# Banded attention and a split-precision feed-forward layer: the planner's port rule, four product parts and single sums

## The chip, the cores and the metric

The kernel runs on one core of one Trainium2 chip. The metric is the device time of one execution in microseconds. Three runs of the kernel before took 921.04, 918.73 and 920.68 us, median 920.68. The engines are TensorE (PE; its weight loads are PEld), VectorE (DVE), ScalarE (ACT), GpSimd (POOL) and SyncE (SP), which issues the DMAs.

## The reference

Attention over a band of 64 keys (8 batches, 8 heads, 576 positions, head size 64), then a feed-forward layer over the 4608 tokens:

```python
scores = scale * np.matmul(q, k.transpose(0, 1, 3, 2))
rel = pos[:, None] - pos[None, :]
scores = np.where((rel >= 0) & (rel < 64), scores, -1000000000.0)
scores = scores - np.max(scores, axis=-1, keepdims=True)
attn = np.exp(scores)
attn = attn / (np.sum(attn, axis=-1, keepdims=True) + 1e-09)
x = np.matmul(attn, v)              # -> (4608, 512)
...
h = x @ w_in                        # (512, 2048)
g = np.where(h >= 1, h, np.where(h <= -1, 0.0, (h + 1) ** 2 / 4))
return g @ w_out                    # (2048, 512)
```

## The kernel before

The tokens are cut into nine tiles of 512. Attention runs in steps of 128 tokens, four to a tile, some tiles ahead of the feed-forward layer. A step is: loads, scores on TensorE (L401), mask (L418) and maximum (L422) on VectorE, exponentials on ScalarE (L429), the inverse of the sum (`den`, L436 and L437) on VectorE, the normalization (`sm`, L441) on VectorE or GpSimd, twelve transposes of 32x32 blocks on VectorE (L447, two times six), and the value product on TensorE (L476).

Matrix operands of the feed-forward layer are split in two: a rounded high part and the low rest, so every product is three matmuls (high x high, high x low, low x high). Tiles 0 and 1 compute h = x w_in directly (L860, one block f of 128 columns of h at a time, 16 blocks to a tile). From tile 2 on (`PLAIN = 2`), two blocks f are computed together as one pair n by seven products of sums in place of eight (L812): sums of parts of x (L529), their high parts (`xs`, L259 casts) and low parts (`xs`, L541), and sums of parts of the weights. The weight sums (`add_sums`, eight of them in two halves c) are computed once, during tile 1: `sum_whole` (L724, two operations), `sum_sums` (L733, four), rounding on ScalarE, `sum_low` (L743). They are written to DRAM (`kept`) and come back for every tile as rings of weights (`wr`, L783).

A pair's products stand in two banks of PSUM, `ps_h`. They were issued in two pieces: 24 matmuls (products 0 to 3), then 18 (products 5, 6 and 4). From the banks, h is put together in SBUF: `h_copy` (L257 or L259) and five sums `h_add` (L828), three after the first piece and two after the second. The second piece waits for the copy and all of the first three sums. The last sum and the last copy free the banks for the next pair. Then, for each block: relu and square on ScalarE (L872, L877; the square on VectorE at times, L879), the gate on VectorE (L884), rounding on ScalarE (`gh`, L889), the low part on GpSimd (`gl`, L894), and twelve matmuls of the second layer (L911) into four `acc` banks.

No order is written out by hand. Every operation is handed to a planner (`Plan.add`) with a key, a cost in ns for each engine that may run it, what it follows, and which buffers it takes and gives back. `Plan.run` plays the kernel forward with these costs: of the operations that an engine could start soonest (within `PATIENCE` of it) it takes the one with the lowest key, and where two engines may run an operation, the one that could start it first gets it. What comes out is each engine's fixed instruction order. The costs are thus no times of the chip but decide the order; `tt(n)` gives those of sums, `hi(n)` those of rounding.

Of the kernel before, what the change touches and what calls it, by code (L numbers as in the profile page):

```python
# [10 lines left out]
F32 = mybir.dt.float32  # L11
# [29 lines left out]
W_LEAD = 0.57  # L41
W_FIRST = (20.54, -1.96, 1.46, 0.57, -0.16)
# [45 lines left out]
S_LATER = 2  # L88
B_KEY = 4 / 3
# [13 lines left out]
class Plan:  # L103
# [9 lines left out]
    def add(self, key, cost, do, after=(), takes=(), gives=(), lag=0):  # L113
        self.work.append((key, cost, do, set(after), takes, gives, lag))
        return len(self.work) - 1
# [16 lines left out]
    def run(self):  # L132
# [9 lines left out]
        turn = dict.fromkeys(self.pools, 0)  # L142

# [8 lines left out]
        for _ in self.work:  # L152
            best = None
            for e in engines:
                could = []
                for i, at in ready[e].items():
                    takes = self.work[i][4]
                    free = [self.pools[n][(turn[n] + takes[:j].count(n)) % len(self.pools[n])] for j, n in enumerate(takes)]
                    if None not in free:
                        could.append((max([at, idle[e]] + free), self.work[i][0], i, e))  # L160
# [5 lines left out]
            _, cost, do, _, takes, gives, lag = self.work[i]  # L166
            idle[e] = self.end(e, at, cost[e])
            ends[i] = idle[e] + lag, e
# [17 lines left out]
def banded_attention_then_ffn(ctx: ExitStack, tc: tile.TileContext, q, k, v, w, masks, out, dims):  # L186
# [142 lines left out]
    def add_weights(f, nf, unit):  # L329
# [3 lines left out]
        key = f * W_STEP - (W_FIRST[f] if f < len(W_FIRST) else W_LEAD) + .5 * nf * unit  # L333
# [217 lines left out]
    def tt(n, k=1):  # L551
        return dict(DVE=100 * k + 1.5 * n, Pool=200 * k + 2.3 * n)

    def hi(n):
        return dict(ACT=90 + .84 * n, DVE=65 + 1.05 * n)

    def add_build(t, r, due, x0, x1):
        i0 = add(due, tt(2 * SB), lambda e: x_sums(t, r, 0, e), [x0, x1], takes=["u"])
        xs = i0
        for j in range(1, 4):  # L560
            xs = add(due, tt(2 * SB), lambda e, j=j: x_sums(t, r, j, e), [xs])
        ends = []
        for k in range(5):
# [6 lines left out]
            x = add(due, hi(n), lambda e, k=k: x_high(t, r, k, e), after, takes=[] if t in x_first else ["x"])  # L570
            x_first.setdefault(t, x)
            gives = [("u", i0)] if k == 1 else [("u", x0)] if k == 4 else []
            x = add(due, tt(n), lambda e, k=k: x_low(t, r, k, e), [x] + ends[-1:], gives=gives)
# [3 lines left out]
    def add_step(t, i):  # L577
# [44 lines left out]
        if s < SOON:  # L622
            for h in range(2):
# [9 lines left out]
                x = add(due + D_LATE[4], NORM[1], lambda e, h=h: att_normalize(s, h, e), [x])  # L633
# [21 lines left out]
        else:  # L655
# [5 lines left out]
            x = [add(due[h], NORM[0], lambda e, h=h: att_normalize(s, h, e), [x]) for h in range(2)]  # L661
# [55 lines left out]
    def sum_whole(n, c, eng):  # L717
        if n < 2:
# [4 lines left out]
        for i, w_ in enumerate(by_chunk(n)):  # L723
            engine[eng].tensor_tensor(  # L724
                out=t[:, 2 * i:2 * i + 2], in0=w_[:, 0, c].bitcast(F32), in1=w_[:, 1, c].bitcast(F32), op=ALU.add
            )

    def sum_sums(n, c, eng):
# [218 lines left out]
    def step(t):  # L947
        return NF * starts[t] / 384
# [180 lines left out]
```

## Time and profile before

The profiled execution took 920.28 us, of which 918.5 are its span.

| what | number |
|---|---|
| median of 3 runs (lowest, highest) | 920.68 us (918.73, 921.04) |
| profiled execution, its span | 920.28 us, 918.5 us |
| granted TensorE clock, mean | 0.987 |
| the chain that ended last | PE 64%, DVE 21%, ACT 6%, DMA 4%, issue 3%, POOL 2% |
| moved by DMA | 187.60 MB, mean 204 GB/s |

How to read the rows: a group of instructions has its line, engine, operation, out<-in, shapes and count, then busy us and mean ns of one, then the idle time before it and what ended it. A row of the timeline has start and length in us, and in brackets the idle time of the engine before it with its releaser. A window has its bounds and length, the busy time of PE, PEld, DVE, ACT and POOL with instruction counts, then the granted clock of TensorE as a share of full speed, the DMA share and GB/s. Lines are those of the kernel before; in the changed kernel the same code stands 8 to 13 lines lower.

### The profile page before, as it was taken

Reading aid. Unit: us, or ns where it says so; the run is one execution under the profiler, and the core shown is the slowest. Engines: PE = TensorE matmul, PEld = TensorE weight load, DVE = VectorE, ACT = ScalarE, POOL = GpSimd, SP = SyncE. Lnnn points to the kernel's source line nnn. Section 1 sums busy time; section 2 is a strip of 40 time slices with the busy share of each in tenths; the row PEclk is TensorE's granted clock in tenths of the full one; section 3 lists DMA queues with packets and bytes.
Section 4 is the critical chain, followed back from the end, with each engine's and each line's share of the span. In section 5 each row is a group of like instructions: output and inputs, shape, how many; then the busy total and the mean of one; then the engine's idle time right before and its main releaser. Section 6 shows DMA issues by size and latency. Waiting matters only on the chain.

```text
span 918.5 us, 20359 instructions
## 1 busy us (share of the span) xinstructions
PE 879.8 (96%) x7839; PEld 762.4 (83%) x7839; DVE 667.5 (73%) x1348; ACT 503.5 (55%) x1297; POOL 317.7 (35%) x305
## 2 busy tenths in 40 slices
PE   7799998989989999999999999999999999999998
PEld 5678886867878888888888898888788878998997
DVE  6999997799787568866787668866895678533331
ACT  7899955455464444644564446435644555434343
POOL 1000035667442425432353235422533343422222
PEclk9999999989998999999999999999999999999999
DMA  9991169366475657655776568556865564556531
GB/s 327 414 364 53 36 203 296 129 208 234 163 240 201 202 189 240 231 183 172 246 230 203 190 208 292 189 174 218 278 197 194 178 229 162 161 164 226 184 116 46
DMA packets 108033, 187.60 MB, mean 204 GB/s; under 512 B 8480, under 2 KB 49696, under 8 KB 107936
## 3 DMA queue, kind: packets, MB, share of 16 engines
q1 hardware_dynamic: 107648, 185.38, 60.5%
q8 instruction: 62, 1.02, 0.5%
q10 hardware_dynamic: 288, 0.92, 0.3%
q14 instruction: 35, 0.29, 0.1%
HBM read 162.15 MB, written 24.12 MB: 203 GB/s over the span
## 4 chain that ended last, share of the span: by engine, by line
PE 64%; DVE 21%; ACT 6%; DMA 4%; issue 3%; POOL 2%; SPq 0%; ACTq 0%; DVEq 0%
PE acc L911 30%; PE ps_h L812 22%; DVE ptd L447 6%; PE ps_h L860 6%; DVE a L884 3%; PE ps_a L476 2%; PE ps_a L401 2%; DVE h L828 2%; ACT a L872 2%; ACT sm L429 2%; DVE xs L259 2%; DVE half L733 2%; DVE u L529 2%; DMA kt<-in_k 2%; DMA kept<-half 1%
## 5 line engine op out<-in xcount | busy, mean ns | idle before, releaser
L911 PE MATMUL acc<-wts,gh 128*128 128x512 f32 x1154 | 363.0, 396 | 0.2 <-ACT o L257 0.2
L812 PEld LDWEIGHTS ps_h<-xs,wr 128*128 128x128 f32 x2352 | 296.1, 191 | 26.4 <-DVE h L828 18.2
L812 PE MATMUL ps_h<-xs,wr 128*128 128x256 f32 x2352 | 304.3, 285 | 14.0 <-DVE h L828 14.0
L894 POOL TENSOR_TENSOR gl<-a,gh 128x512 fp32r<-128x512 f32 (+1 forms) x130 | 171.1, 1320 | 316.2 <-ACT gh L889 299.2
L911 PEld LDWEIGHTS acc<-wts,gh 128*128 128x128 f32 x1154 | 208.3, 189 | 41.2 <-ACT o L257 0.6
L911 PE MATMUL acc<-wts,gl 128*128 128x512 f32 x577 | 225.2, 390 | 0.3 <-POOL gl L894 0.3
L828 DVE TENSOR_TENSOR h<-h,ps_h 128x256 f32<-128x256 f32 x280 | 116.7, 417 | 109.7 <-PE ps_h L812 80.8
L889 ACT CAST gh<-a 128x512 fp32r<-128x512 f32 (+1 forms) x149 | 89.6, 602 | 122.9 <-PE acc L911 93.2
L447 DVE STREAM_TRANSPOSE ptd<-sm 32x256 f32<-32x256 f32 x336 | 146.3, 435 | 8.0 <-POOL sm L441 2.2
L911 PEld LDWEIGHTS acc<-wts,gl 128*128 128x128 f32 x577 | 108.9, 189 | 24.5 <-POOL gl L894 0.7
L884 DVE SCALAR_TENSOR_TENSOR a<-a,h 128x512 f32<-128x512 f32 x112 | 86.5, 772 | 57.9 <-ACT a L877 56.9
L429 ACT ACTIVATE sm<-sm,nm 128x96 f32<-128x96 f32 (+1 forms) x256 | 93.1, 365 | 49.0 <-DVE nm L422 49.0
L860 PE MATMUL ps_h<-xh,wts 128*128 128x512 f32 (+1 forms) x296 | 91.9, 379 | 10.1 <-DVE a L884 7.8
L257 ACT COPY h<-ps_h 128x256 f32<-128x256 f32 x95 | 35.3, 371 | 118.5 <-PE ps_h L812 118.2
L877 ACT ACTIVATE a<-a 128x512 f32<-128x512 f32 (+1 forms) x140 | 86.3, 617 | 4.4
L872 ACT ACTIVATE a<-h 128x512 f32<-128x512 f32 x112 | 70.0, 625 | 10.2 <-DVE h L828 10.2
L860 PEld LDWEIGHTS ps_h<-xh,wts 128*128 128x128 f32 x296 | 55.4, 195 | 22.3 <-DVE a L884 9.6
L541 POOL TENSOR_TENSOR xs<-u,xs 128x256 fp32r<-128x256 f32 (+1 forms) x57 | 60.0, 1075 | 23.7 <-DVE xs L259 22.0
L724 POOL TENSOR_TENSOR half<-wts 128x256 f32<-128x256 f32 x18 | 13.5, 769 | 132.7 <-PE ps_h L860 126.6
L860 PE MATMUL ps_h<-xl,wts 128*128 128x512 f32 (+1 forms) x148 | 55.5, 375 | 0.9 <-DVE xl L489 0.9
L441 POOL TENSOR_TENSOR sm<-sm,den 128x384 f32<-128x384 f32 x30 | 32.3, 1082 | 66.3 <-DVE den L437 62.2
L429 ACT ACTIVATION_READ_ACCUMULATOR sm<-sm,nm 128x1 f32 x256 | 48.0, 188 | 0.0
(89 smaller groups left out, 763.8 us busy)
## 6 DMA issues: line engine op xcount, KB each, us to landing
wr<-kept SPq DMA_DIRECT2D x112, 512.0 KB, 4.6
wr<-kept SPq DMA_DIRECT2D x112, 384.0 KB, 3.8
vt<-in_v SPq DMA_DIRECT2D x72, 256.0 KB, 4.0
kt<-in_k SPq DMA_DIRECT2D x35, 384.0 KB, 5.4
raw<-in_w SPq DMA_DIRECT2D x12, 1023.8 KB, 10.3
qt<-in_q SPq DMA_DIRECT2D x36, 256.0 KB, 4.9
out<-o SPq DMA_DIRECT2D x33, 256.0 KB, 4.7
kept<-wts SPq DMA_DIRECT2D x48, 128.0 KB, 2.5
```

The costliest lines, as they stand in the source:

```text
L429: nc.scalar.activation(sm[:, p, :], (ps if masked else sm)[:, p, :], AF.Exp, bias=nm[:, p:p + 1], scale=scale if masked else 1.0, accum_ou ...
L447: nc.vector.transpose(dst[:, :, r], src[:, :, c * SQ:(c + 1) * SQ])
L541: engine[eng].tensor_tensor(out=x_target(t, r, k, 1), in0=x_source(t, r, k), in1=x_target(t, r, k, 0).bitcast(F32), op=ALU.subtract)
L812: nc.tensor.matmul(ps[:, c * 2 * SB:(c + 1) * 2 * SB], lhsT=r[:, part, cp, o], rhs=xo[k][:, xp, cp], start=i == 0 and c == 0 and j == 0 an ...
L828: nc.vector.tensor_tensor(out=h[:, to:to + 256], in0=h[:, of:of + 256], in1=ps[:, at:at + 256], op=ALU.add)
L860: nc.tensor.matmul(ps, lhsT=wts[f, 0][:, part, c * P:(c + 1) * P], rhs=x[:, c, r], start=(c == 0 and j == 0), stop=(c == NP - 1 and j == 2),)
L872: nc.scalar.activation(gs[t, f, r.start][0], phs[t, f, r.start], AF.Relu, bias=0.5, scale=0.5)
L877: nc.scalar.activation(a, a, AF.Square)
L884: nc.vector.scalar_tensor_tensor(out=a, in0=a, scalar=1.0, in1=ps, op0=ALU.min, op1=ALU.max)
L889: nc.scalar.copy(g[1], g[0])
L894: engine[eng].tensor_tensor(out=g[2], in0=g[0], in1=g[1].bitcast(F32), op=ALU.subtract)
L911: nc.tensor.matmul(acc[t, i][:, n], lhsT=g[:, sub], rhs=wts[f, 1][:, part, n], start=(q == 0 and j == 0), stop=(q == NF - 1 and j == 2 and ...
```

## The change

1. The planner gets a resource that VectorE and GpSimd share. Every GpSimd operation holds it, and every VectorE operation that is added with `shared=True`: sums of x, their high and low parts, normalizations of attention, squares, gates of tiles from 2 on, and the weight sums. Two holders don't overlap in the plan. The costs change with it: VectorE's sums from 100 + 1.5 n to 65 + 1.04 n ns, its rounding from 65 + 1.05 n to 30 + 0.6 n, the gate from 100 + 1.3 n to 65 + 1.04 n, GpSimd's sums from 2.3 n to 2.15 n.
2. The products of a pair come in four parts of 12, 12, 6 and 12 matmuls. The third part needs the copy and the first sum of h, the fourth all three. The third part is now product 4 (bank 0) alone, so the last copy follows it and not the last part.
3. `sum_whole` and `sum_sums` become six operations for the planner in place of two; the instructions are the same.
4. Three keys change: the second-layer weights of joint loads (`W_PAIR`), the pace of the weight sums (`S_PACE`, 2 for a sum in place of 2.67), and that of the third part (`X_KEY`).

```diff
+W_PAIR = 0, 2.0
+S_PACE = 2
+X_KEY = 1.3
...
     def run(self):
...
+        held = 0.0
...
                     if None not in free:
+                        if e == "Pool" or e == "DVE" and self.work[i][7]:
+                            free.append(held)
                         could.append((max([at, idle[e]] + free), self.work[i][0], i, e))
...
             idle[e] = self.end(e, at, cost[e])
+            if e == "Pool" or e == "DVE" and shared:
+                held = idle[e]
...
-        key = f * W_STEP - (W_FIRST[f] if f < len(W_FIRST) else W_LEAD) + .5 * nf * unit
+        key = f * W_STEP - (W_FIRST[f] if f < len(W_FIRST) else W_LEAD) + (W_PAIR[unit] if nf == 2 else .5 * unit)
...
     def tt(n, k=1):
-        return dict(DVE=100 * k + 1.5 * n, Pool=200 * k + 2.3 * n)
+        return dict(DVE=65 * k + 1.04 * n, Pool=200 * k + 2.15 * n)
 
     def hi(n):
-        return dict(ACT=90 + .84 * n, DVE=65 + 1.05 * n)
+        return dict(ACT=90 + .84 * n, DVE=30 + .6 * n)
...
-            x = [add(due[h], NORM[0], lambda e, h=h: att_normalize(s, h, e), [x]) for h in range(2)]
+            x = [add(due[h], NORM[0], lambda e, h=h: att_normalize(s, h, e), [x], shared=True) for h in range(2)]
...
-        key = step(1) + 2 * n * TMAX / 384 + (S_LATE if n < 2 else S_LATER)
+        key = step(1) + S_PACE * n + (S_LATE if n < 2 else S_LATER)
...
-            k = key + c * TMAX / 384
-            x0 = add(k, tt(2 * TMAX // 2, 2), lambda e, c=c: sum_whole(n, c, e), after, takes=["tmp"])
+            k = key + c * S_PACE / 2
+            xs = add(k, tt(2 * P), lambda e, c=c: sum_whole(n, c, 0, e), after, takes=["tmp"], shared=True)
+            x0 = add(k, tt(2 * P), lambda e, c=c: sum_whole(n, c, 1, e), [xs], shared=True)
...
-            x = add(k, tt(4 * P, 4), lambda e, c=c: sum_sums(n, c, e), [x0])
+            x = x0
+            for j in range(4):
+                x = add(k, tt(P), lambda e, c=c, j=j: sum_sums(n, c, j, e), [x], shared=True)
...
         todo = (
-            ((a, 0, 0, 0), (a, 1, 1, 1), (b, 0, 2, 2), (b, 1, 3, 3)),
-            ((b, 0, 2, 5), (b, 1, 0, 6), (a, 0, 1, 4)),
+            ((a, 0, 0, 0), (a, 1, 1, 1)), ((b, 0, 2, 2), (b, 1, 3, 3)), ((a, 0, 1, 4),), ((b, 0, 2, 5), (b, 1, 0, 6))
         )[i]
...
+        xa = add(key, dict(PE=12 * pe), lambda e: ffn_products(t, n, 0), needs, takes=["ps_h", "ps_h", "h"])
+        ya = add(key, dict(PE=12 * pe), lambda e: ffn_products(t, n, 1), [xa], gives=[("ra", ra)])
         m = [add(key, take, lambda e: h_copy(t, n, 512, e), [xa])]
...
+        m.append(add(key, cost, lambda e: h_add(t, n, 256, 512, 0, 256), m[-1:]))
+        for v in (768, 256, 1, 0), (768, 768, 1, 256):
+            m.append(add(key, cost, lambda e, v=v: h_add(t, n, *v), [ya, m[-1]]))
+        xb = add(key + X_KEY, dict(PE=6 * pe), lambda e: ffn_products(t, n, 2), [rb, ya, *m[:2]])
+        yb = add(
+            key + B_KEY, dict(PE=12 * pe), lambda e: ffn_products(t, n, 3), [xb, *m],
             gives=[("rb", rb)] + [("x", x_first[t])] * (n == NF // 2 - 1),
         )
+        xm = add(key, take, lambda e: h_copy(t, n, 0, e), [xb], gives=[("ps_h", xa, 0)])
+        xl = add(key, cost, lambda e: h_add(t, n, 512, 256, 1, 0), [yb])
```

**Where it moves instructions.** First TensorE, from tile 2 to tile 3 (the same at later tile changes): a new tile's first pair. `ps_h<-xs,wr` are the products, `acc` the second layer, `ps_a<-kt,qt` the scores. Before:

```order
L812 MATMUL ps_h<-xs,wr 128x256 x24
L911 MATMUL acc<-wts,gh 128x512 x2
L911 MATMUL acc<-wts,gl 128x512
L911 MATMUL acc<-wts,gh 128x512 x2
L911 MATMUL acc<-wts,gl 128x512
L401 MATMUL ps_a<-kt,qt 32x96 x32
L911 MATMUL acc<-wts,gh 128x512 x2
L911 MATMUL acc<-wts,gl 128x512
L911 MATMUL acc<-wts,gh 128x512 x2
L911 MATMUL acc<-wts,gl 128x512
L812 MATMUL ps_h<-xs,wr 128x256 x18
```

The same place in the change:

```order
L824 MATMUL ps_h<-xs,wr 128x256 x24
L924 MATMUL acc<-wts,gh 128x512 x2
L924 MATMUL acc<-wts,gl 128x512
L924 MATMUL acc<-wts,gh 128x512 x2
L924 MATMUL acc<-wts,gl 128x512
L824 MATMUL ps_h<-xs,wr 128x256 x6
L409 MATMUL ps_a<-kt,qt 32x96 x32
L824 MATMUL ps_h<-xs,wr 128x256 x12
```

Six matmuls of the second layer now stand behind the products, and the scores between the third and the fourth part. A value product with three second-layer matmuls on either side stands ahead of the 24 in the change; before, it stood ahead with three behind it. Elsewhere in a tile the order is 24, twelve of the second layer, 18, with scores behind the 18 and value products behind the 24.

At the same place VectorE, before (`h<-h,ps_h` are the sums of h, `u` sums of x, `xs` its high and low parts, `a` gates):

```order
L828 TENSOR_TENSOR h<-h,ps_h 128x256
L259 CAST xs<-u 128x2x2x128
L828 TENSOR_TENSOR h<-h,ps_h 128x256
L259 CAST xs<-u 128x2x128 x2
L828 TENSOR_TENSOR h<-h,ps_h 128x256
L418 SCALAR_TENSOR_TENSOR sm<-ps_a,nmsk 128x384 x2
L422 TENSOR_REDUCE nm<-sm 128x8
```

and in the change:

```order
L455 STREAM_TRANSPOSE ptd<-sm 32x8x32 x12
L840 TENSOR_TENSOR h<-h,ps_h 128x256 x2
L267 COPY u<-ps_a 128x512
L897 SCALAR_TENSOR_TENSOR a<-a,h 128x512
L537 TENSOR_TENSOR u<-u 128x256
L892 TENSOR_TENSOR a<-a 128x512
L840 TENSOR_TENSOR h<-h,ps_h 128x256
L537 TENSOR_TENSOR u<-u 128x256
L897 SCALAR_TENSOR_TENSOR a<-a,h 128x512
L537 TENSOR_TENSOR u<-u 128x256
L840 TENSOR_TENSOR h<-h,ps_h 128x256 x2
L267 COPY h<-ps_h 128x256
```

The three casts between the sums of h are gone to ScalarE; sums of x and gates stand there instead, and behind these rows masks, maximum and sums of h follow without an operation that holds the port. Twelve transposes stand in one row behind two normalizations. GpSimd does one sum of x, one `gl` and four low parts here; before it did two, one and five.

In tile 1, where the first x of the new form is built, VectorE before:

```order
L541 TENSOR_TENSOR xs<-u,xs 128x2x2x128
L259 CAST xs<-u 128x2x128
L441 TENSOR_TENSOR sm<-sm,den 128x384
L724 TENSOR_TENSOR half<-wts 128x256 x2
L884 SCALAR_TENSOR_TENSOR a<-a,ps_h 128x512
```

and in the change (`half` are sums of weights):

```order
L549 TENSOR_TENSOR xs<-u,xs 128x2x2x128
L267 CAST xs<-u 128x2x128
L549 TENSOR_TENSOR xs<-u,xs 128x2x2x128
L897 SCALAR_TENSOR_TENSOR a<-a,ps_h 128x512
L753 TENSOR_TENSOR half<-half,o 128x512
L549 TENSOR_TENSOR xs<-u,xs 128x2x128
L734 TENSOR_TENSOR half<-wts 128x256
```

The gate stands ahead of the normalization and of the weight sums, which are spread singly.

Over the whole program, VectorE does 56 normalizations of 128x384 in place of 28 and GpSimd 2 in place of 30; sums of x on VectorE go from 38 to 44, low parts from 13 to 25, casts of xs from 32 to 15, copies of h from 17 to 35.

More of the change, by code (lines that the diff above doesn't have):

```diff
@@ L111, in __init__, with add @@
         self.columns = {}
-    def add(self, key, cost, do, after=(), takes=(), gives=(), lag=0):
-        self.work.append((key, cost, do, set(after), takes, gives, lag))
+    def add(self, key, cost, do, after=(), takes=(), gives=(), lag=0, shared=False):
+        self.work.append((key, cost, do, set(after), takes, gives, lag, shared))
         return len(self.work) - 1
@@ L165, in run @@
             at, _, i, e = best
-            _, cost, do, _, takes, gives, lag = self.work[i]
+            _, cost, do, _, takes, gives, lag, shared = self.work[i]
             idle[e] = self.end(e, at, cost[e])
+            if e == "Pool" or e == "DVE" and shared:
+                held = idle[e]
             ends[i] = idle[e] + lag, e
```

61 lines of the change are left out of this document (27 added, 34 removed).

## The prediction

> **What bounds the kernel now.** I read the busy time by engine first, then the table of windows, then what TensorE waited for, then the rows around each wait.
>
> ```profile
> span 918.5 us, 20359 instructions
> PE 879.8 (96%) x7839; PEld 762.4 (83%) x7839; DVE 667.5 (73%) x1348; ACT 503.5 (55%) x1297; POOL 317.7 (35%) x305
> ...
> 44.00:140.00 96.00, 95.92 (x709) 77.57 (x709) 94.11 (x177) 79.51 (x158) 8.12 (x11) 1.00 0.49 166
> ...
> 188.00:202.00 14.00, 10.32 (x33) 7.83 (x32) 12.85 (x25) 7.42 (x20) 9.77 (x12) 0.76 0.45 146
> ...
> 262.00:285.00 23.00, 18.33 (x184) 16.22 (x183) 20.21 (x42) 11.27 (x32) 10.81 (x9) 0.85 0.67 226
> ...
> 356.00:452.40 96.40, 93.96 (x916) 83.03 (x912) 72.41 (x145) 49.44 (x136) 36.57 (x31) 1.00 0.66 214
> ...
> 741.00:756.50 15.50, 13.58 (x192) 11.41 (x190) 12.21 (x19) 8.97 (x29) 9.44 (x9) 0.89 0.69 225
> ...
> 798.50:903.00 104.50, 104.18 (x656) 94.21 (x655) 35.14 (x71) 43.31 (x82) 25.74 (x20) 1.00 0.50 159
> ```
>
> TensorE (PE) is the bound: 96% busy, and full in the weight stage (44 to 140 us) and the last tile (798 to 903). What can be gained is its idle time between those, and the clock that is lost after it: the column behind the busy times is the granted clock, 0.76, 0.85 and 0.89 in three windows and 1.00 in the others. The rows of its waits say who ends them.
>
> ```profile
> PE ps_h L812 <- DVE h L828: 14.0, 10, 3.5
> PE ps_h L860 <- DVE a L884: 7.8, 3, 3.7
> ...
> 147.77 0.39 PE L860 MATMUL ps_h<-xh,wts 128*128 128x256 f32 x1 [1.97 <-DVE a L884]
> 195.35 0.79 PE L860 MATMUL ps_h<-xh,wts 128*128 128x512 f32 x1 [3.68 <-DVE a L884]
> 263.93 1.15 PE L476 MATMUL ps_a<-ptd,vt 128*64 128x64 f32 x32 [1.13 <-DVE sm L418]
> 277.53 2.72 PE L812 MATMUL ps_h<-xs,wr 128*128 128x256 f32 x11 [3.54 <-DVE h L828]
> 365.69 1.55 PE L812 MATMUL ps_h<-xs,wr 128*128 128x256 f32 x11 [1.94 <-DVE h L828]
> ...
> 750.32 1.88 PE L812 MATMUL ps_h<-xs,wr 128*128 128x256 f32 x10 [1.92 <-DVE h L828]
> ```
>
> All end on VectorE (DVE). Ten waits of the products (L812) for the sums of h (L828) take 14.0 us: 3.54 once, about 1.9 at each tile change but one (the first, at 365.69, and the last, at 750.32, are shown), 0.5 at smaller places. Tile 1 adds 3.68 + 1.97, a wait of the value products (L476) 1.13. Together 14.0 + 5.65 + 1.13 = 20.8 us. The clock lost, at most: 0.24 x 14 + 0.15 x 23 + 0.11 x 15.5 = 3.4 + 3.4 + 1.7 = 8.5 us. **What could come back is 29.3 us.** The waits before 140 us lie in a part whose order hardly changes; I leave them.
>
> Why VectorE is late shows at 362 us, beside an earlier place where GpSimd (POOL) rests:
>
> ```profile
> 360.89 0.87 DVE L529 TENSOR_TENSOR u<-u 128x256 f32<-128x256 f32 x2
> ...
> 362.67 2.63 DVE L259 CAST xs<-u 128x256 fp32r<-128x256 f32 x2
> 365.23 0.41 DVE L828 TENSOR_TENSOR h<-h,ps_h 128x256 f32<-128x256 f32 x1
> ...
> 362.57 4.72 POOL L541 TENSOR_TENSOR xs<-u,xs 128x512 fp32r<-128x512 f32 x5 [2.16 <-DVE xs L259]
> ...
> 269.68 0.45 DVE L259 CAST xs<-u 128x256 fp32r<-128x256 f32 x2
> ```
>
> Two casts that take 0.45 us while POOL rests (269.68) take 2.63 while it runs five operations in a row: 2.2 us, longer than TensorE's wait of 1.94, and the third sum of h stands right behind them. At 191 us it is the same:
>
> ```profile
> 190.51 0.92 DVE L259 CAST xs<-u 128x256 fp32r<-128x256 f32 x1
> 191.35 1.62 DVE L441 TENSOR_TENSOR sm<-sm,den 128x384 f32<-128x384 f32 x1
> 192.90 1.80 DVE L724 TENSOR_TENSOR half<-wts 128x256 f32<-128x256 f32 x2
> 194.62 0.68 DVE L884 SCALAR_TENSOR_TENSOR a<-a,ps_h 128x512 f32<-128x512 f32 x1
> ...
> 191.24 4.04 POOL L541 TENSOR_TENSOR xs<-u,xs 128x512 fp32r<-128x512 f32 x4
> ```
>
> The gate (L884) that frees the bank is last in a queue of blocked operations.
>
> **The change part by part.** The prices:
>
> ```profile
> L828 DVE TENSOR_TENSOR h<-h,ps_h 128x256 f32<-128x256 f32 x280 | 116.7, 417 | 109.7 <-PE ps_h L812 80.8 <-ACT h L257 24.0
> L418 DVE SCALAR_TENSOR_TENSOR sm<-ps_a,nmsk 128x384 f32<-128x384 f32 x58 | 30.2, 551 | 7.7 <-PE ps_a L401 7.7
> L441 DVE TENSOR_TENSOR sm<-sm,den 128x384 f32<-128x384 f32 x28 | 23.6, 850 | 0.5
> L436 DVE TENSOR_SCALAR den<-den 128x8 f32<-128x8 f32 x28 | 8.9, 319 | 8.7 <-ACT sm L429 8.6
> L436 DVE TENSOR_SCALAR den<-den 128x4 f32<-128x4 f32 x16 | 2.7, 166 | 0.3 <-ACT sm L429 0.3
> L441 POOL TENSOR_TENSOR sm<-sm,den 128x384 f32<-128x384 f32 x30 | 32.3, 1082 | 66.3 <-DVE den L437 62.2
> L894 POOL TENSOR_TENSOR gl<-a,gh 128x512 fp32r<-128x512 f32 x126 | 167.7, 1335 | 313.9 <-ACT gh L889 296.9 <-PE acc L911 8.1 <-PE ps_a L476 4.3
> 347.74 2.23 DVE L447 STREAM_TRANSPOSE ptd<-sm 32x256 f32<-32x256 f32 x5
> L812 PEldq EVENT_SEMAPHORE  x110: 51/51/51, 248.0 to 898.1; - x110
> ```
>
> *Port as a resource.* No instruction is added; the order moves. 28 of POOL's 30 normalizations (L441, 1.08 us each) go to VectorE, with six sums of x and ten low parts more there. On VectorE a normalization takes about the 0.55 us of the mask operation of the same shape (L418), so 28 x 0.55 = 15 us are added to an engine busy 667.5 of 918.5; they lie beside TensorE's work except where a transpose and a value product stand behind them (term b). POOL's gl don't come sooner for it: it idles 296.9 us for ScalarE's rounding ahead of them. At a tile change the order puts the sums of h, the copy, masks and the maximum beside POOL's burst; the sums of h keep 417 ns in 280 mixed places, so they should run through it.
>
> *Four parts.* 12 + 12 + 6 + 12 matmuls for 24 + 18: as many, in the same time. The copy of h can start half a part, 2.85 / 2 = 1.4 us, earlier:
>
> ```profile
> 292.26 2.15 PE ps_h L812 x18
> 294.41 2.75 PE acc L911 x12
> 297.16 2.85 PE ps_h L812 x24
> ...
> 361.16 1.00 PE L401 MATMUL ps_a<-kt,qt 64*32 64x96 f32 x64
> ...
> L257 ACT COPY h<-ps_h 128x256 f32<-128x256 f32 x95 | 35.3, 371 | 118.5 <-PE ps_h L812 118.2
> ```
>
> Between 24 and 18 usually stand 12 matmuls of the second layer (2.75). Before, copy and three sums (0.37 + 3 x 0.42 = 1.6 us) began when the 24 ended: 1.1 us to spare. Now two sums are left then (0.8): 1.9 to spare. Two parts more in each of 56 pairs can bring 112 more semaphore waits of 51 ns on TensorE's queue: 0 to 5.7 us; most lie in front of busy matmuls, I take **1**.
>
> *Sums as single operations; keys.* The counts stay, so the cost is nothing by itself; DMAs and their number stay too, and SP's queue keeps the order of ring loads within a tile. Gates can now pass between the sums. Later keys for the second-layer weights fall in the full stage (95.92 of 96): nothing to gain, up to 2 us to lose; I take 0.
>
> **What comes back late**, in four terms:
> (a) Tile change. Behind the value product VectorE has a copy, two gates and a square (0.68 each, as the gate at 194.62), three sums of x (0.87 / 2 each) and three of h (0.42): 2.7 + 1.3 + 1.3 = 5.3 us. TensorE reaches the fourth part after 0.7 (three matmuls of the second layer) + 2.85 + 1.4 (six) + 0.7 (the third part) + 1.00 (scores) = 6.6. So 1.3 to spare, which one gl of POOL (1335 ns) uses up and a second turns into a wait; I take 0.5 x 5 = **2.5**, bounds 0 and the 8.5 of before (5 of at most 1.94).
> (b) Value products. Two normalizations and twelve transposes in a row take 1.1 + 12 x 0.446 = 6.5 us. At the tile change they start 1.2 us after the 24 (sums, inverse), end at 7.7, and the value product comes at 2 x 2.75 + 2.15 + 0.7 = 8.3: 0.6 to spare, less than one block by POOL. 23 of them stand in the product stage: 0 to 1.3 each; I take 0.2, nearer the 1.13 us in all of before: **4.6**.
> (c) Tile 1. Ahead of the gate at 194.62 stood, behind the first low part of x, a cast, a normalization and two sums of weights: 194.62 - 190.51 = 4.1 us. In the order now a cast and one more low part stand there, 0.92 + 0.68 (by the gate's shape) = 1.6: the gate comes 2.5 earlier, and of 3.68 some 1.2 stays; of the 1.97 I leave 0.6: **1.8**, bounds 0 and 5.65. The wait of 1.94 left the clock at 1.00 (row of 356 to 452.4), so I count no clock with these.
> (d) Start of tile 2. 24, scores, 18 in a row stand there still, with 1.00 of cover between: I leave **1** of 3.54 + 1.13 = 4.7, bounds 0 and 4.7.
> Sum: 1 + 2.5 + 4.6 + 1.8 + 1 = 10.9. Net 29.3 - 10.9 = 18.4 us. From the profiled execution's 920.28 us (its span 918.5 and 1.8 around it; 0.4 under the median of 920.68): **901.9 us**.
>
> The L436 rows show what the plan leaves out: 319 ns beside POOL, 166 for the early ones. The Trainium skill, "SBUF — State Buffer", section "Who interferes with whom", says why: tensor_scalar can enter a two-port mode and then contends, and the inverse is not marked as shared. The trace agrees; by that rule up to 28 x 0.153 = 4.3 us more would come back, an estimate of 906.2.
> On the clock, the row of 741 to 756.5 has 0.89 after a wait of 1.92. The Trainium skill, "TensorE: Matmul & The Clock Gate", Part 1, has the clock halved after an idle window of about 3.4 us. By it a wait of 1.92 costs nothing and the gain is 1.7 less, 903.6; the row disagrees.
>
> **The rivals.**
> *Half of it (912.2).* Value products wait 0.5 us each (11.5 in place of 4.6) and one clock loss of 3.4 stays: 920.28 - 29.3 + 6.3 (the other terms) + 11.5 + 3.4. For it: the 0.6 us to spare in (b). Against: before, the one of 1.13 is the only wait of a value product over 1 us after 140 us.
> *Slower: the value products.* If a gl (1.3 us) blocks each pair of normalizations, TensorE waits about 1.3 at all 23: 29.9 against the 29.3 - 6.3 = 23.0 left: 927.2. It decides from 23.0 / 23 = 1.0 us each. For it: 850 ns mean of L441 on VectorE. Against: POOL has 28 x 1.08 = 30 us less to do.
> *The plan isn't kept (920).* Nothing in the instructions holds POOL back; if its gl drift into the same places, the waits come again elsewhere: 918 to 923.
>
> **How the numbers follow.** Forecast 0.62 (891 to 907), half 0.22 (907 to 917), plan not kept 0.08, slower 0.08. The range takes all of the 29.3 us at its lower end and most of the half case: 891 to 916. 0.3% is about 2.8 us, what a measurement of this kernel tells from no change: faster 0.84, within 0.08, slower 0.08.
>
> **What would show it.** The products' wait for h falls from 14.0 to under 4 us; the granted clock is 1.00 from 140 us to the end; a tile (96.4 us, the window of 356 to 452.4) falls to about 94; casts of xs on VectorE stay near 0.25 us each; L441 on VectorE has x56 at under 650 ns. I am wrong if L476 waits for transposes sum to over 10 us, or if VectorE's share near 190 us still ends in a wait of TensorE for a gate.

## The result, and the profile after

| kernel | median us (lowest to highest, runs) | profiled execution, its span |
|---|---|---|
| before | 920.07 (918.73 to 921.04, 4) | 920.28, 918.5 |
| the change | 906.88 (906.34 to 907.99, 4) | 907.99, 906.2 |

The ratio is 0.9859, with a 95% interval from 0.9842 to 0.9876: 13.2 us faster, where 18.4 were forecast. The time is right to 5 us, but taken by stages the forecast is off by more than that in two places, in opposite directions. 906.88 also lies at the upper end of the stretch called likeliest (891 to 907), next to the rival of half the gain.

The head of the page after the change, span and busy time by engine:

```profile
span 906.2 us, 20363 instructions
...
PE 875.5 (97%) x7839; PEld 762.9 (84%) x7839; DVE 656.1 (72%) x1391; ACT 506.8 (56%) x1291; POOL 264.2 (29%) x268
```

TensorE was idle for 918.5 - 879.8 = 38.7 us before and for 906.2 - 875.5 = 30.7 now. GpSimd gave up 53.5 us of work and VectorE still has 11.4 less, since fewer of its operations are blocked and more casts of `xs` run on ScalarE.

What TensorE waits for, in us in total, times, longest:

```profile
PE ps_h L873 <- DVE a L897: 6.6, 3, 3.9
PE ps_h L873 <- DVE xh L267: 4.1, 2, 2.6
PE acc L924 <- ACT o L265: 2.7, 1, 2.7
PE ps_a L484 <- DVE ptd L455: 2.5, 6, 0.4
...
PE ps_h L824 <- DVE h L840: 0.3, 1, 0.3
```

The products' wait for h, 14.0 us in ten places before, is 0.3 in one. The first three rows now lead, and all three belong to the direct products and the second layer of tiles 0 and 1; before, these waits were 7.8, 2.2 and 0.2. The value products wait 0.4 us once in each of six tiles, midway between two tile changes. One of them stands at 404 us, between the tile changes near 357 and 451:

```profile
404.85 1.03 PE L484 MATMUL ps_a<-ptd,vt 128*64 128x64 f32 x28 [0.42 <-DVE ptd L455]
```

Windows of the change (bounds, length, busy time of PE, PEld, DVE, ACT, POOL, granted clock, DMA share, GB/s):

```profile
44.00:140.00 96.00, 96.00 (x715) 78.11 (x715) 92.87 (x172) 77.98 (x157) 8.41 (x13) 1.00 0.47 163
140.00:240.00 100.00, 88.87 (x799) 70.88 (x794) 76.14 (x161) 50.88 (x148) 51.31 (x66) 0.93 0.64 214
240.00:340.00 100.00, 99.25 (x892) 87.44 (x892) 77.41 (x166) 51.87 (x139) 32.18 (x31) 0.97 0.61 204
340.00:906.20 566.20, 560.43 (x5046) 500.86 (x5044) 373.86 (x799) 290.20 (x739) 169.43 (x143) 1.00 0.61 201
349.00:443.00 94.00, 93.58 (x914) 83.50 (x913) 70.23 (x152) 50.61 (x136) 29.28 (x25) 1.00 0.67 219
...
188.00:202.00 14.00, 14.00 (x62) 11.17 (x61) 13.84 (x28) 10.16 (x28) 7.13 (x8) 1.00 0.38 132
```

and of the kernel before in the same stages:

```profile
140.00:240.00 100.00, 92.62 (x765) 73.60 (x760) 85.02 (x163) 54.56 (x155) 64.99 (x77) 0.97 0.63 213
240.00:340.00 100.00, 94.76 (x983) 83.62 (x982) 71.55 (x152) 48.21 (x134) 36.40 (x30) 0.97 0.61 197
340.00:918.50 578.50, 564.05 (x4993) 500.31 (x4991) 382.01 (x767) 286.03 (x742) 205.29 (x172) 1.00 0.61 198
```

A tile in the product stage went from 96.40 to 94.00 us. From 140 to 240 us the change is worse: 11.1 us idle for 7.4, at a clock of 0.93 for 0.97.

Since the stages hold slightly different work, a fairer measure counts it: every matmul that starts in a stretch is taken at its usual spacing at full clock (0.1196 us for a product, 0.2285 for the second layer, and so on; the same prices for all kernels), and the sum is taken off the stretch. What is left is lost time, idle or slow; only its differences between kernels mean something. From one profiled execution each, and good to some 2 us, since the prices taken for attention's many small matmuls move it by that:

```
lost us                    140-240  240-340  340-end
before                        11.0      9.4     22.5
the change                    16.1      4.6     10.0
gain, measured                -5.1      4.8     12.5
gain, by the forecast          7.2      7.1      4.1
```

The last row sorts the prediction's own terms by place: tile 1 (5.65 - 1.8, and 3.4 of clock at 188), start of tile 2 (4.7 - 1, and 3.4 of clock at 262), the rest (14.0 - 3.54, 1.7 of clock, less 2.5, 4.6 and 1). So the product stage gave 8.4 us more than forecast and tile 1 some 12 less.

**Tile 1.** The timeline of the change, from where the first x of tile 1 is needed (SPq is SP's queue with its DMA issues; L734 builds weight sums and L753 their low parts, L723 copies parts of the weights to DRAM, L758 and L759 store a finished sum, L265 and L267 are copies and casts):

```profile
122.47 14.10 SPq L723 DMA_DIRECT2D kept<-wts  x24
131.95 1.29 POOL L753 TENSOR_TENSOR half<-half,o 128x512 fp32r<-128x512 f32 x1
136.54 0.60 ACT L265 CAST o<-half 128x512 fp32r<-128x512 f32 x1
137.21 0.40 SPq L759 DMA_DIRECT2D kept<-half  x1
...
141.64 0.42 DVE L734 TENSOR_TENSOR half<-wts 128x256 f32<-128x256 f32 x1 [1.78 <-DMA kept<-half]
142.58 0.68 DVE L267 CAST xh<-ps_a 128x512 fp32r<-128x512 f32 x1
143.32 0.58 PE L873 MATMUL ps_h<-xh,wts 128*128 128x256 f32 x1 [2.60 <-DVE xh L267]
143.51 3.34 SPq L723 DMA_DIRECT2D kept<-wts  x6
146.95 0.42 SPq L758 DMA_DIRECT2D kept<-o  x1
150.05 0.58 ACT L265 COPY o<-acc 128x512 f32<-128x512 f32 x1 [7.19 <-DMA kept<-o]
150.69 1.22 PE L924 MATMUL acc<-wts,gh 128*128 128x512 f32 x2 [2.65 <-ACT o L265]
...
239.74 0.79 PE L873 MATMUL ps_h<-xh,wts 128*128 128x512 f32 x1 [3.90 <-DVE a L897]
```

There are two buffers for weight sums and two for `o`, which holds rounded sums and outputs. VectorE's weight sum at 141.64, the third, waits until the first stored sum has left its buffer, and the cast of x (142.58) stands behind it: TensorE waits 2.60 us. That stored sum was ready at 133.24 and issued at 137.21, behind 24 copies that took SP 14.10 us. ScalarE's copy at 150.05 has waited 7.19 us for a buffer `o` that the second rounded sum (136.54) took; its DMA was issued at 146.95, behind six copies that took 3.34 us: TensorE waits 2.65. The third, at 239.74, is the gate's old wait in a new place.

The clock of TensorE beside that, in the same 16 us of the change and of the kernel before (granted clock in the column behind POOL's time):

```profile
140.00:156.00 16.00, 9.95 (x57) 7.88 (x52) 9.54 (x19) 6.06 (x23) 9.12 (x14) 0.60 0.97 300
```

```profile
140.00:156.00 16.00, 12.57 (x88) 9.90 (x83) 12.47 (x28) 10.01 (x31) 8.26 (x12) 1.00 0.98 317
```

57 matmuls in place of 88, at a clock of 0.60 in place of 1.00. The half clock lasts from 143.2 to 156.9 us.

### The profile page after: what moved, and what is told of

Read it like the earlier page. It is cut to its first block, busy times and chain, and to the rows that moved or that the text cites. A ratio compares the mean times of both kernels' runs of the same rounds, so it can differ in the third digit from the quotient of the medians.

```text
span 906.2 us, 20363 instructions
## 1 busy us (share of the span) xinstructions
PE 875.5 (97%) x7839; PEld 762.9 (84%) x7839; DVE 656.1 (72%) x1391; ACT 506.8 (56%) x1291; POOL 264.2 (29%) x268
## 4 chain that ended last, share of the span: by engine, by line
PE 75%; DVE 12%; DMA 5%; ACT 3%; issue 2%; SPq 2%; POOL 0%; ACTq 0%; DVEq 0%
PE acc L924 36%; PE ps_h L824 27%; PE ps_h L873 6%; DVE ptd L455 4%; PE ps_a L484 3%; PE ps_a L409 3%; DVE a L897 2%; DMA kept<-half 2%; DMA kt<-in_k 2%; SPq L723 1%; ACT a L885 1%; DVE h L840 1%; DVE sm L449 1%; DVE half L734 1%; DVE half L743 1%
## 5 line engine op out<-in xcount | busy, mean ns | idle before, releaser
L824 PE MATMUL ps_h<-xs,wr 128*128 128x256 f32 x2352 | 299.2, 282 | 0.3 <-DVE h L840 0.3
L907 POOL TENSOR_TENSOR gl<-a,gh 128x512 fp32r<-128x512 f32 (+1 forms) x130 | 167.6, 1290 | 427.5 <-ACT gh L902 389.7
L437 ACT ACTIVATE sm<-sm,nm 128x96 f32<-128x96 f32 (+1 forms) x256 | 93.0, 365 | 12.2 <-DVE nm L430 12.1
L265 ACT COPY h<-ps_h 128x256 f32<-128x256 f32 x77 | 28.7, 372 | 47.3 <-PE ps_h L824 43.6
L549 POOL TENSOR_TENSOR xs<-u,xs 128x256 fp32r<-128x256 f32 (+1 forms) x45 | 42.3, 971 | 32.0 <-ACT xs L265 32.0
L734 POOL TENSOR_TENSOR half<-wts 128x256 f32<-128x256 f32 x12 | 9.4, 790 | 140.1 <-PE ps_h L873 123.7
L484 PEld LDWEIGHTS ps_a<-ptd,vt 128*64 128x64 f32 x992 | 32.0, 137 | 13.1 <-DVE ptd L455 3.6
```

The lines of the kernel that those rows point to most:

```text
L437: nc.scalar.activation(sm[:, p, :], (ps if masked else sm)[:, p, :], AF.Exp, bias=nm[:, p:p + 1], scale=scale if masked else 1.0, accum_ou ...
L484: nc.tensor.matmul(ps[half[h], p, n], lhsT=vt[i][:, c:c + D], rhs=pt[h][:, p, n], start=True, stop=True)
L824: nc.tensor.matmul(ps[:, c * 2 * SB:(c + 1) * 2 * SB], lhsT=r[:, part, cp, o], rhs=xo[k][:, xp, cp], start=i < 2 and c == 0 and j == 0 and ...
L907: engine[eng].tensor_tensor(out=g[2], in0=g[0], in1=g[1].bitcast(F32), op=ALU.subtract)
```

## The experiments

Each kernel is the changed one with the edit shown, unless said otherwise; each was timed beside the kernel before (919.92 us beside the first four, 920.25 beside the next four, 920.32 beside the last four). The lost time of all of them, counted as above (the median stands beside it; a profiled execution can lie up to 3.8 us from it, as in 3):

```
lost us                          140-240  240-340  340-end   median us
before                              11.0      9.4     22.5     920.1
the change                          16.1      4.6     10.0     906.9
1 old pace                          10.3     14.3     10.0     912.4
2 no port rule                      20.9     10.9     17.4     927.5
3 two parts                         15.6      7.7      9.4     906.9
4 port rule and costs only           6.7     16.9      9.3     912.5
5 SP dearer                          9.7      5.1     10.0     902.5
6 W_PAIR undone                      8.3      2.2     10.0     898.8
7 sums joined                        8.7      7.8     10.0     905.5
8 gates earlier                     11.3      8.1      9.4     906.7
9 before, with W_PAIR               13.5      9.4     23.5     924.7
10 W_PAIR undone, SP dearer          6.4      1.4      9.5     896.6
11 W_PAIR undone, two parts          8.5      3.5      9.9     898.0
12 W_PAIR undone, old pace           6.0     15.7     10.2     908.6
```

**1. The old pace.**

```diff
-        key = step(1) + S_PACE * n + (S_LATE if n < 2 else S_LATER)
+        key = step(1) + 8 / 3 * n + (S_LATE if n < 2 else S_LATER)
-            k = key + c * S_PACE / 2
+            k = key + c * 4 / 3
```

> The changed kernel with the pace of the weight sums put back to 8/3 a sum and 4/3 a half. In the changed kernel tile 1 has a new wait of 2.6 us (behind a weight sum that waits for a DMA), one of 2.65 (an output copy behind a DMA) and one of 3.9 (a gate with 24 VectorE operations ahead of it), and 20.5 us at half clock. Theory A, the faster pace puts sums and their DMAs ahead of gates: the gate's wait and the DMA waits go, 894 to 902 us against 906.9, and a tile of products stays at 94.0 us. Rival, the single sums or the port rule crowd tile 1: 904 to 909.

Measured: 912.40 us (911.90 to 915.80, 5 runs), ratio 0.9930 [0.9902, 0.9958], 5.5 us slower than the change and outside both expectations. The gate's wait of 3.90 us is gone, but the waits at 140 to 152 us stay (2.5 and 3.1), and the start of tile 2 becomes worse, which the table shows (4.6 to 14.3). So the faster pace is no cause of the loss at 140 us, and it earns its place later.

**2. Without the port rule.** Costs, parts and keys of the change are kept.

```diff
-                        if e == "Pool" or e == "DVE" and self.work[i][7]:
-                            free.append(held)
```

> The changed kernel with costs, four parts, single sums and keys kept, but the planner without the shared resource (operations no longer wait for its holder in the plan). Theory A, the port rule brings the gain in the product stage: TensorE's waits for sums of h come back (5 to 14 us in all), a tile takes 95 to 96.5 us, the whole 914 to 922. Rival, the four parts bring it: a tile stays at 94.0 and the whole at 904 to 909.

Measured: 927.51 us (926.82 to 931.83, 4 runs), ratio 1.0098 [1.0068, 1.0128]: slower than before, and 20.6 us slower than the change, which is theory A's side but beyond its range. A tile's window and two rows of TensorE's waits without the rule:

```profile
390.00:485.40 95.40, 94.13 (x914) 83.28 (x913) 73.45 (x150) 49.23 (x133) 36.36 (x31) 1.00 0.66 216
```

```profile
PE ps_h L871 <- DVE a L895: 16.6, 4, 6.5
...
PE ps_h L822 <- DVE h L838: 2.6, 6, 0.4
```

A tile takes 95.40 us in place of 94.00, and the gates of tile 1 are waited for 16.6 us in place of 6.6. The waits for sums of h come back to 2.6 us only, not to theory A's 5 to 14; by the table 7.4 of the 20.6 us are lost from 340 us on, the rest before. The rule carries the gain of the change, and more than that.

**3. Two parts.** The products in 24 and 18 again, everything else of the change.

```diff
-        xa = add(key, dict(PE=12 * pe), lambda e: ffn_products(t, n, 0), needs, ...)
-        ya = add(key, dict(PE=12 * pe), lambda e: ffn_products(t, n, 1), [xa], ...)
+        xa = add(key, dict(PE=24 * pe), lambda e: [ffn_products(t, n, i) for i in range(2)], needs, ...)
...
-        xb = add(key + X_KEY, dict(PE=6 * pe), lambda e: ffn_products(t, n, 2), [rb, ya, *m[:2]])
-        yb = add(key + B_KEY, dict(PE=12 * pe), lambda e: ffn_products(t, n, 3), [xb, *m], ...)
+        xb = add(key + B_KEY, dict(PE=18 * pe), lambda e: [ffn_products(t, n, i) for i in (3, 2)], [rb, xa, *m], ...)
```

> The changed kernel with the products in two pieces of 24 and 18 again. Theory A, the port rule does it: a tile takes 94.0 to 94.6 us, at most 0.5 us of wait at a tile change, the whole 905 to 911. Rival, the four parts are needed: waits of over 1 us at each tile change, a tile 95.5 to 96.5, the whole 915 to 922.

Measured: 906.91 us (904.78 to 910.70, 4 runs), ratio 0.9869 [0.9837, 0.9900], the same as the change, as theory A had it. A tile of it:

```profile
400.00:493.60 93.60, 93.60 (x915) 83.36 (x914) 69.95 (x149) 51.41 (x140) 29.21 (x25) 1.00 0.67 220
```

With two parts a tile takes 93.60 us with TensorE full; with four it takes 94.00 with 93.58 busy. The waits that the four parts were to shorten are gone without them. The 0.4 us that a tile takes longer with four parts are the one wait of its value product shown above (0.42): from 300 us on no value product waits as long in the kernels with two parts and the port rule (3, 4 and 11), and in all with four parts some do.

**4. The port rule and the costs alone.** Old pace, old W_PAIR, sums joined as in 7, two parts as in 3.

> The kernel before with the port rule and the new costs alone: products in two pieces, weight sums joined, all keys as before. Theory A: product tiles of about 94.2 us and no crowding in tile 1, 902 to 908 us. Rival, the parts or the single sums carry the gain: 913 to 921.

Measured: 912.47 us (910.94 to 914.50, 4 runs), ratio 0.9926 [0.9902, 0.9951]. The time lies in neither expectation's range, though the product tiles are those of theory A: the product stage has its whole gain (9.3 us lost; tile 93.60) and tile 1 loses 6.7 us, less than before, but the start of tile 2 loses 16.9. No run has the new costs alone; in 2, which keeps them without the rule, they bring no gain.

**5. SP's transfers dearer to the planner.** It sees six issues (L723) as 3.6 us, and the two of a stored sum as 0.9.

```diff
-        xp = add(key, dict(SP=1600), lambda e: sum_pass(n), ready + [x_in[0]], lag=DMA_LAG)
+        xp = add(key, dict(SP=3600), lambda e: sum_pass(n), ready + [x_in[0]], lag=DMA_LAG)
-            x = add(k, dict(SP=1500), lambda e, c=c: sum_keep(n, c), [x], lag=DMA_LAG, ...)
+            x = add(k, dict(SP=900), lambda e, c=c: sum_keep(n, c), [x], lag=DMA_LAG, ...)
```

> The changed kernel with the planner's SyncE costs of the weight sums as the trace has them: 3600 in place of 1600 for the six DMAs of a sum's copies, 900 in place of 1500 for the two that store a sum. Theory A, at 140 to 152 us TensorE waits because a stored sum's DMA stands behind six others on SyncE's queue (value sums 2.6, output copy 2.65, gate 0.65, and some 6.8 us of clock): these go, no half clock between 140 and 160 us, 896 to 902 us against 906.9. Rival, the waits there come from other work of VectorE and ScalarE: 904 to 909 with the same waits.

Measured: 902.46 us (900.97 to 905.46, 4 runs), ratio 0.9809 [0.9779, 0.9839], 4.4 us faster than the change; 140 to 240 us loses 9.7 in place of 16.1. The half clock shrinks from 13.7 + 6.8 to 3.4 + 3.4 us. The costs are now near those of the trace (3.34 to 4.78 us for six issues in the change), and the order shows what they do:

```profile
123.13 7.43 SPq L723 DMA_DIRECT2D kept<-wts  x12
133.95 0.33 SPq L759 DMA_DIRECT2D kept<-half  x1
...
138.54 0.92 DVE L734 TENSOR_TENSOR half<-wts 128x256 f32<-128x256 f32 x1
143.75 0.68 DVE L267 CAST xh<-ps_a 128x512 fp32r<-128x512 f32 x1
```

The stored sum stands behind 12 copies instead of 24, and VectorE's weight sum, still ahead of the cast of x, doesn't wait for it. A wait of 2.81 us for an output copy stays at 142 to 145 us, so the time is just above theory A's range.

**6. W_PAIR undone.**

```diff
-        key = ... + (W_PAIR[unit] if nf == 2 else .5 * unit)
+        key = ... + .5 * nf * unit
```

> The changed kernel with the key of the second-layer weights (W_PAIR) put back. Theory A, that key moves the weight stage's end and with it the waits at 140 to 152 us (the kernel with the port rule alone, with the old key, has one wait of 2.5 there and no half clock): they shrink to 2 to 4 us, 899 to 904 us. Rival, the key does nothing there: 905 to 909.

Measured: 898.76 us (897.38 to 899.33, 4 runs), ratio 0.9762 [0.9738, 0.9787], 8.1 us faster than the change. Its timeline at the place of the loss, and the window:

```profile
121.01 18.45 SPq L723 DMA_DIRECT2D kept<-wts  x30
140.32 0.38 SPq L759 DMA_DIRECT2D kept<-half  x1
...
141.88 0.69 DVE L267 CAST xh<-ps_a 128x512 fp32r<-128x512 f32 x1 [0.94 <-PE ps_a L484]
142.78 1.42 POOL L734 TENSOR_TENSOR half<-wts 128x256 f32<-128x256 f32 x2 [2.29 <-DMA kept<-half]
...
150.39 0.62 ACT L265 CAST o<-half 128x512 fp32r<-128x512 f32 x1 [0.79 <-DMA out<-o]
```

```profile
140.00:156.00 16.00, 12.80 (x87) 10.39 (x86) 11.71 (x26) 9.13 (x29) 7.63 (x11) 0.89 1.01 329
```

The first stored sum leaves even later here (140.32, behind 30 copies). But the third weight sum, which waits for it, stands on GpSimd (142.78); on VectorE the cast of x stands behind no weight sum and waits only for its own value product. ScalarE rounds the second sum at 150.39, not at 136.54, so that sum holds no `o` while outputs are copied. TensorE runs 87 matmuls in the 16 us, as before the change (88). Theory A holds, and the time is even 0.2 us under its range.

**7. Sums joined.** `sum_whole` and `sum_sums` as two operations of the planner again.

```diff
-            xs = add(k, tt(2 * P), lambda e, c=c: sum_whole(n, c, 0, e), after, takes=["tmp"], shared=True)
-            x0 = add(k, tt(2 * P), lambda e, c=c: sum_whole(n, c, 1, e), [xs], shared=True)
+            xs = x0 = add(k, tt(4 * P, 2), lambda e, c=c: [sum_whole(n, c, i, e) for i in range(2)], after, ...)
...
-            for j in range(4):
-                x = add(k, tt(P), lambda e, c=c, j=j: sum_sums(n, c, j, e), [x], shared=True)
+            x = add(k, tt(4 * P, 4), lambda e, c=c: [sum_sums(n, c, j, e) for j in range(4)], [x0], shared=True)
```

> The changed kernel with the weight sums joined again (two and four operations planned as one), pace 2 kept. Theory A, single sums let gates pass, so without them TensorE waits longer for gates in tile 1: 908 to 914 us. Rival, single sums are what crowds the gate at 236 us (24 VectorE operations ahead of it; here 22): 902 to 906.

Measured: 905.51 us (905.38 to 906.13, 4 runs), ratio 0.9839 [0.9815, 0.9863]. That is the rival's range. With the new W_PAIR no gain hangs on the single sums: the joined ones are 1.4 us quicker, and the intervals overlap. No run has them joined with W_PAIR undone and the new pace.

**8. The gates of tile 1 earlier.**

```diff
-                    key + late[2], dict(DVE=65 + n * 1.04), lambda e, f=f, r=r: ffn_gate(t, f, r), ...
+                    key + late[2] - 4 * (t == 1), dict(DVE=65 + n * 1.04), lambda e, f=f, r=r: ffn_gate(t, f, r), ...
```

> The changed kernel with the keys of tile 1's gates 4 lower, so that they go ahead of weight sums and sums of x. Theory A, the wait of 3.9 us at 236 us and its 6.8 us of half clock come from the gate's place alone: both go, 7 us less, 898 to 902 us. Rival, the work that the gate passes is late next (as with the old pace, where value products at the start of tile 2 waited 7.7 and 3.5 us): 904 to 913.

Measured: 906.66 us (906.58 to 908.46, 4 runs), ratio 0.9857 [0.9827, 0.9887], as the change and as the rival had it. The wait of 3.90 us for a gate is gone, and at 241 us the second layer waits 3.9 us for a `gl` in its place; the waits at 140 to 152 us stay.

**9. The kernel before, with the new W_PAIR alone.**

```diff
-        key = ... + .5 * nf * unit
+        key = ... + (2.0 * unit if nf == 2 else .5 * unit)
```

> The kernel before, with one line of the change: the term added to W_PAIR. Theory A (the key alone delays the first tiles, since the pairs' inverses and products stand later whatever the rest of the plan is): 922 to 928 us against 920, and new waits of PE between 128 and 160 us. Rival B (the key costs only together with the other order, in which the product stage leaves fewer slots for the pairs): 917 to 923 us, no new wait there.

Measured: 924.72 us (922.09 to 926.18, 10 runs), ratio 1.0043 [1.0027, 1.0058], 4.4 us slower than before. Theory A holds in time and place. The same waits as in the change, in a kernel without the port rule:

```profile
124.18 18.61 SPq L715 DMA_DIRECT2D kept<-wts  x30
...
143.43 0.41 SPq L749 DMA_DIRECT2D kept<-half  x1
...
145.93 0.76 DVE L724 TENSOR_TENSOR half<-wts 128x256 f32<-128x256 f32 x2 [4.97 <-DMA kept<-half]
147.21 0.68 DVE L259 CAST xh<-ps_a 128x512 fp32r<-128x512 f32 x1
147.94 0.58 PE L860 MATMUL ps_h<-xh,wts 128*128 128x256 f32 x1 [5.51 <-DVE xh L259]
```

Thirty copies (18.61 us) stand ahead of the stored sum's issue; the weight sum waits 4.97 us for it on VectorE, a copy and the cast of x stand behind it, and TensorE waits 5.51. In the kernel before the same matmul waited little: the stored sum was issued earlier, and VectorE's weight sum stood behind the cast:

```profile
120.00 17.61 SPq L715 DMA_DIRECT2D kept<-wts  x30
...
139.93 0.38 SPq L749 DMA_DIRECT2D kept<-half  x1
...
140.88 0.69 DVE L259 CAST xh<-ps_a 128x512 fp32r<-128x512 f32 x1 [0.76 <-PE ps_a L476]
141.62 0.38 PE L860 MATMUL ps_h<-xh,wts 128*128 128x256 f32 x1 [0.79 <-DVE xh L259]
...
145.16 1.12 DVE L724 TENSOR_TENSOR half<-wts 128x256 f32<-128x256 f32 x2 [0.98 <-DMA kept<-half]
```

So with the new key a weight sum that waits for a stored sum stands ahead of the cast of x in 1, 3, 7, 8 and 9 and in the change, and with the old key in none (before, 4, 6, 10, 11, 12). In 2 it doesn't either, but there an output copy on VectorE waits 5.73 us for one. Why the plan moves it so stays open.

**10. W_PAIR undone, and SP's transfers dearer** (6 and 5 together).

> The changed kernel with W_PAIR as before, and with the planner's costs of SP's transfers raised (pass 3600, keep 900 ns). Theory A (what is left at tiles 1 and 2 is still SP's queue, so the two edits add up): 893 to 898 us. Rival B (both edits mend the same waits): 898 to 903 us.

Measured: 896.59 us (895.02 to 902.98, 4 runs), ratio 0.9761 [0.9713, 0.9810]. The median falls where theory A has it, but the ratio is that of 6 (0.9762), and the four runs spread over 8 us. Whether the costs of SP bring anything once W_PAIR is undone stays open; the medians differ by 2.2 us.

**11. W_PAIR undone, two parts** (6 and 3 together; 24 and 18 matmuls).

> The changed kernel with W_PAIR as before, and the products in 24 and 18 columns again. Theory A (four parts bring nothing, now that the other wait is away as well): 897 to 901 us. Rival B (the shorter wait of four parts counts once W_PAIR no longer covers it): above 903 us.

Measured: 897.97 us (896.12 to 901.13, 4 runs), ratio 0.9757 [0.9724, 0.9790], the same as 6. Theory A holds: four parts bring nothing here either.

**12. W_PAIR undone, old pace** (6 and 1 together).

> The changed kernel with W_PAIR as before, and S_PACE as before too. Theory A (the pace is worth what it was worth with the new W_PAIR, some 5 us, at the start of tile 2): about 904 us, and waits of the value products between 247 and 262 us. Rival B (the pace only mattered because the weights' order was late): 897 to 900 us.

Measured: 908.62 us (906.67 to 910.48, 4 runs), ratio 0.9869 [0.9838, 0.9899]. Rival B falls, and theory A had the place right and the size half: the pace is worth 9.9 us here. Window and wait of this kernel at the start of tile 2:

```profile
240.00:262.00 22.00, 15.02 (x211) 12.15 (x209) 19.54 (x42) 11.52 (x40) 9.28 (x14) 0.77 0.73 254
```

```profile
PE ps_a L484 <- DVE ptd L455: 7.0, 7, 3.3
```

TensorE is busy for 15.02 of 22 us at a clock of 0.77. In 6, with the new pace, the same window is full at 0.97:

```profile
240.00:262.00 22.00, 22.00 (x247) 19.64 (x246) 16.86 (x39) 10.32 (x19) 7.42 (x8) 0.97 0.66 207
```

The faster pace takes the weight sums out of VectorE's queue before the first value products of tile 2 need it.

Read as one path, each step a run: before 920.1, port rule and costs 912.5 (4), with four parts and single sums 908.6 (12), with the new pace 898.8 (6), with the new W_PAIR 906.9. The steps don't add up in another order: without the rule the same keys and parts make the kernel slower (2). The 3.9 us between 4 and 12 stay open: the tests of four parts (3, 11) and of single sums (7) show no gain, and the profiled executions of 4 and 12 took 910.94 and 910.48 us.

## Why the prediction was right, and where it was wrong

- **The port rule, and what could come back.** Right in mechanism. All 12.2 us that the prediction named from 340 us on (14.0 - 3.54 of waits for h, 1.7 of clock) came back: no wait for h is left there, and the clock is 1.00. Lost time fell from 22.5 to 10.0, and experiments 2 and 4 show that rule and costs alone do it. The normalization on VectorE takes 563 ns in 56 places (0.55 taken), and the eight casts of 128x256 that VectorE keeps 285 ns:

```profile
L840 DVE TENSOR_TENSOR h<-h,ps_h 128x256 f32<-128x256 f32 x280 | 117.5, 420 | 127.8 <-PE ps_h L824 113.0 <-ACT h L265 8.0
L449 DVE TENSOR_TENSOR sm<-sm,den 128x384 f32<-128x384 f32 x56 | 29.3, 563 | 0.9
```

  These are groups of the change (busy us, mean ns). The sums of h, at 420 ns as before, do run through GpSimd's work.
- **(a) and (b), 2.5 and 4.6 us back.** Too much. The products wait 0.3 us and the value products 2.5, six times 0.4, each midway in a tile; the other 17 of the 23 show no wait. At the tile change, the place that the prediction worked out, its 0.6 us to spare held. 0.2 us for each of 23 places was a price without a row.
- **Four parts, 1 us.** A small cost was right by another cause: 0.4 us a tile (94.00 to 93.60 with two parts), which is no row of semaphore waits on TensorE but the value product's wait, the same 2.5 us as above. Their gain is zero, in 3 and in 11. With two parts and the port rule the products' waits for h are already down to some 1 us in all (3), so the longer slack of 1.9 us had nothing left to cover.
- **Keys, "nothing to gain, up to 2 us to lose; I take 0".** This is the step that failed. The full stage (95.92 of 96) still is full (96.00), but behind it the new order has VectorE's third weight sum ahead of the cast of x, where it waits for a stored sum, and the stored sum's DMA stands behind 24 to 30 copies on SP's queue. "SP's queue keeps the order of ring loads within a tile" says nothing of these stores. The loss needs both: with the old key the cast comes first (6), with SP's copies priced as in the trace the store comes early (5), and either way TensorE no longer waits for x behind a stored sum. Cost: 8.1 us in the change (6), 4.4 in the kernel before (9). Undone, the change gains 21.3 us.
- **(c) Tile 1, 1.8 us.** The gate near 190 us did come in time (14.00 of 14.00 busy). But weight sums of the faster pace stand ahead of a gate at 239 us, for which TensorE waits 3.90 (gone with the old pace, in 1), and moving the gates (8) only turns that into a wait for `gl`. With rule and costs alone (4) tile 1 lost 4.3 us less than before, of 7.2 forecast with the clock. I took one place of the new order for the stage.
- **"I count no clock with these."** Wrong. The sign that the prediction gave for it, a clock of 1.00 from 140 us on, fails: 13.7 us of half clock at 143.2 and 6.8 at 238.8. At the end of the waits of 2.60 and 3.90 us the clock halved, after the value products' 0.4 it didn't. The prediction's other signs came.
- **(d) Start of tile 2, 1 us back.** Near in size, 4.8 us measured against 7.1 with its clock, but by another cause, and so luck: rule and costs alone make this stretch worse (9.4 to 16.9 lost, in 4). The prediction gave S_PACE no share; 1 and 12 show that the gain hangs on it (5.5 and 9.9 us).
- **The rivals.** Value products late by 0.5 or 1.0 us at all 23 places didn't come (0.4 at six). The plan did reach the chip: without its rule the time is 20.6 us longer (2).
- **The inverse.** In the Trainium skill, "SBUF — State Buffer", section "Who interferes with whom", tensor_scalar can contend with GpSimd, and from that I estimated 4.3 us still lost in the inverse. Its rows went from 319 to 183 ns though the plan doesn't mark it. The traces show why: before, 10 of the 28 ran beside a GpSimd operation, and 7 of these took 661 to 1276 ns; in the change 1 does, with 683, and the other 27 take 157 to 173. The order moved GpSimd's work away from it by itself.
- **The sum.** 18.4 us forecast, 13.2 measured. That it lies in the range is in part luck: the product stage gave 8.4 us more than forecast and tile 1 some 12 less.

## What to carry to other kernels

Where a planner or a queue order is changed, follow each moved key to every in-order queue that its results feed, and ask what stands there behind an operation that waits for a buffer and which DMA issue frees it: a key moved inside a full stage cost 8 us behind that stage. Test each edit of a bundle alone and on top of the others: here one rule carried the gain, the pace gave 5.5 to 9.9 us beside it, two edits showed no gain, and one key took 8 us back. And split the forecast by stage, not only by cause, since a total can be right by two errors that cancel.

## What the runs showed of the hardware

- A short wait can cost more through the clock than by itself. In the change a wait of 2.60 us and one of 2.65, 5 us apart, left TensorE at half clock for 13.7 us without a break. With W_PAIR undone a single wait of 2.70 us cost 3.4 us of half clock; in the kernel before the waits of about 1.9 us left it at full rate, except the last one at 750 us. The stretches at half clock last 3.4, 6.8, 10.2 or 13.7 us in all runs, apart from the last of each run, which its end cuts off. In 4 a single wait of 2.36 us left the clock at full rate, so the length of a wait alone doesn't decide. The Trainium skill, "TensorE: Matmul & The Clock Gate", Part 1, has the clock halved after an idle window of about 3.4 us; the length of the stretches agrees, but here waits shorter than that were at times enough.
- Small DMA issues fill SP's queue: six of 128 KB each (by the page's list of DMA issues) took 3.12 (5) to 4.83 us (3) in a row, 24 took 14.10 and thirty 17.61 (before) and 18.61 (9), and a buffer's release waited behind them.
- With two parts and the port rule (3) TensorE had no idle time left in a tile: 93.60 us busy of 93.60.
